# Row scatters tied to TensorE's updates, the expert counts moved by one first product, and a split of the last scaled tile, in a one-core retention + mixture-of-experts kernel

## The chip, the cores and the metric

The kernel runs on one core of a Trainium2 chip. The metric is the device time of one execution in microseconds (us); the lower the better. The engines are TensorE (PE in the profile, its weight loads PEld), VectorE (DVE), ScalarE (ACT), GpSimd (POOL) and SyncE (SP), which here only starts transfers. The kernel's code calls them T, V, A, G and SP.

## The reference, cut to what matters

```python
# q, k, v: [8, 8, 576, 64]
scores = scale * q @ k.transpose(0, 1, 3, 2)
Dmat = where(rel >= 0, gamma[head] ** rel, 0)        # rel = pos_i - pos_j
x = ((scores * Dmat) @ v) -> [4608, 512]             # heads side by side in a row
...
logits = x @ w_gate                                  # 8 experts
e_idx = argmax(logits);  gate_w = softmax(logits)[e_idx]
eom = sigmoid(x @ w_output_gate)
for e in range(8):
    m = e_idx == e
    out[m] = gate_w[m] * eom[m, e] * (relu(x[m] @ w1[e]) @ w2[e])   # F = 1024
```

Every row of x goes through one expert alone, the one with the largest logit.

## The kernel before

The attention works through 36 tiles of 128 rows (NTILE), all heads at once; the loop over g in the manual schedule writes down the order of the instructions of each engine. For tile g TensorE runs: `scores(g + 1)` (32 products of 64x64 on the diagonal block), `by_state(g)` (16 products of the queries with the state that stands for all earlier rows), `outT(g)` (16 products of the masked scores with the values, added to the same PSUM bank `o_ps`), `update(g)` (16 products that add the tile to the state), for about half the tiles `k_rows(g + 1)` (4 transposes), and `xnat(g - 1)` (8 products that turn the tile's result to rows of x and its logits). One tile in nine is without by_state (it begins a sequence), one without update (it ends one).

Beside it VectorE masks the scores (`S_sb`, L384), scales the result (`xT`, L427), does the gate (`gate1a` to `gate4`, for groups of GT = 4 tiles) and part of the split of the weights in two fp32r halves (L153). ScalarE copies the state (`stT`, L402), the keys and the rows of x (`xgrp`, L546) out of PSUM. GpSimd has two things to do in a tile: `prep(g + 1)` (the values scaled by the decay, `vp`, L360), and one indirect DMA of 128 finished rows of x from `xgrp` to their expert's place in `xs` in device memory (`scatter_x`, L200). The scatters of a group stand in the list `todo`; `scatters(n, pause)` takes the next n off it and puts a memset of a 1x1 tile `gap` (L588) ahead of each. That memset is there to wait for GpSimd's own earlier work. Since GpSimd takes its instructions in order, a scatter starts when prep ahead of it is done and its rows are there.

After the tiles come the experts, 8 of them, in two parts of slots each. `mm1(e, part, fb)` makes one block of 128 hidden units: `mm1_products` is 12 products (4 blocks of the inner size, three products of the fp32r halves each) into `h_ps` (L268), `hidden` is relu on ScalarE (L275) and the low half on VectorE (L276). `mm2(e, t)` makes 128 rows of y in `y_ps` by 24 products of 512 columns (L289), ScalarE scales them by the gate (L294) and GpSimd scatters them to the output (L295). Around the end of the attention the counts of rows per expert are made: VectorE finishes `cum` (L518), one small product sums it over partitions (`c_ps`, L734, tile t_ps), and from the copy `cnt` (L735) VectorE works out which slots of `xs` stay empty; GpSimd then fills those with zeros, by scatters with the tile `fill` (L743 and L200).

`pe[0]` is a variable that holds one TensorE instruction; some loads wait for it (`read(paced=...)`). Before, only mm1 and mm2 set it.

## Time and profile before

| what | value |
|---|---|
| median of 3 runs | 603.05 us (602.06 to 604.78) |
| the profiled execution | 606.21 us |
| its span in the trace | 604.40 us |
| TensorE busy | 593.0 us of the span (98%) |
| granted TensorE clock, mean | 0.997 |
| attention | about 0 to 159 us |
| first expert's first blocks, gate of the last group, counts | 159 to 175 us |
| experts | to 597 us |
| last rows scaled and scattered | 597.4 to 600.9 us |

The profile shows one execution on one core. "Busy" of TensorE is modelled from the starts of the products: a stall inside a run of short products shows less in the busy time than in the time from one group's start to the next group's. In the timeline, a row is a run of like instructions: start, length, engine, line, operation, what is written and read, shapes, how many, and in brackets the idle time of that engine before it with what ended it ("issue" where the profile shows no cause).

### The profile page before, as it was taken

The page shows a single profiled execution, that of the slowest core. Times are in us where ns is not written, and L with a number is a line of the kernel's source. Part 1 is how long each engine was busy: PE and PEld are TensorE (multiplying, and loading weights), DVE is VectorE, ACT ScalarE, POOL GpSimd, SP SyncE. Part 2 cuts the span into 40 slices and gives each one's busy share as a digit, 9 for nine tenths or more (in the row PEclk, how much of TensorE's full clock was granted, in tenths as well). Part 3 has the DMA queues.
Part 4 walks back from the last instruction along what each step waited for, and adds up shares of the span by engine and source line. Part 5 has one row for each costly group of instructions (what it writes and reads, how often), then busy time and mean ns, then how long its engine had stood idle before and what let it go on. Part 6 is the DMA issues. An engine that isn't in the chain of part 4 may idle for free. (4 is left out here: it accounts for less than half of the span.)

```text
span 604.4 us, 14010 instructions
## 1 busy us (share of the span) xinstructions
PE 593.0 (98%) x5692; PEld 530.2 (88%) x5692; DVE 330.5 (55%) x731; ACT 226.0 (37%) x502; POOL 189.1 (31%) x235
## 2 busy tenths in 40 slices
PE   8999999999999999999999999999999999999995
PEld 6888888888988999889979987997899799889974
DVE  3588788889650765625543563445265435626410
ACT  4534333234422544325332533443354234325110
POOL 2255454575565624116014301601340110110011
PEclk9999999999999999999999999999999999999998
DMA  8888889887226576435243634434362435221011
GB/s 315 303 307 297 318 300 329 301 278 237 91 106 190 169 207 178 145 102 158 94 133 117 175 109 145 120 122 140 98 192 88 134 96 146 94 84 52 1 39 41
DMA packets 54429, 98.97 MB, mean 164 GB/s; under 512 B 14903, under 2 KB 33336, under 8 KB 54364
## 3 DMA queue, kind: packets, MB, share of 16 engines
q1 hardware_dynamic: 44492, 75.42, 39.2%
q0 software_dynamic: 9440, 21.60, 9.7%
q8 instruction: 45, 0.74, 0.5%
q10 hardware_dynamic: 432, 1.05, 0.4%
q14 instruction: 20, 0.16, 0.1%
HBM read 76.45 MB, written 31.18 MB: 178 GB/s over the span
## 5 line engine op out<-in xcount | busy, mean ns | idle before, releaser
L268 PE MATMUL h_ps<-xh,w1h 128*128 128x360 f32 (+1 forms) x512 | 155.3, 303 | 0.0
L268 PE MATMUL h_ps<-xh,w1l 128*128 128x360 f32 (+1 forms) x512 | 155.0, 303 | 0.0
L268 PE MATMUL h_ps<-xl,w1h 128*128 128x360 f32 (+1 forms) x512 | 154.9, 303 | 0.0
L295 POOL DMA_INDIRECT out_dram<-y,idx x40 | 39.7, 993 | 314.1 <-ACT y L294 268.9
L276 DVE SCALAR_TENSOR_TENSOR hl<-h_ps,hh 128x360 fp32r<-128x360 f32 (+1 forms) x128 | 61.2, 478 | 127.9 <-ACT hh L275 112.5
L289 PE MATMUL y_ps<-w2h,hh 128*128 128x512 f32 (+1 forms) x320 | 124.9, 390 | 0.0
L289 PE MATMUL y_ps<-w2l,hh 128*128 128x512 f32 (+1 forms) x320 | 124.9, 390 | 0.0
L289 PE MATMUL y_ps<-w2h,hl 128*128 128x512 f32 (+1 forms) x320 | 124.6, 389 | 0.0
L275 ACT ACTIVATE hh<-h_ps 128x360 fp32r<-128x360 f32 (+1 forms) x128 | 54.7, 428 | 118.5 <-PE h_ps L268 113.1
L268 PEld LDWEIGHTS h_ps<-xl,w1h 128*128 128x128 f32 x512 | 96.3, 188 | 0.3
L268 PEld LDWEIGHTS h_ps<-xh,w1h 128*128 128x128 f32 x512 | 96.0, 188 | 0.3
L268 PEld LDWEIGHTS h_ps<-xh,w1l 128*128 128x128 f32 x512 | 96.0, 188 | 0.0
L294 ACT ACTIVATE y<-y_ps,idx 128x512 f32<-128x512 f32 (+1 forms) x40 | 27.5, 688 | 138.5 <-issue 90.1
L289 PEld LDWEIGHTS y_ps<-w2h,hl 128*128 128x128 f32 (+1 forms) x320 | 58.8, 184 | 14.1
L289 PEld LDWEIGHTS y_ps<-w2h,hh 128*128 128x128 f32 (+1 forms) x320 | 58.8, 184 | 13.8
L153 DVE TENSOR_TENSOR w1l<-st,w1h 128x512 fp32r<-128x512 f32 x64 | 44.5, 732 | 48.0 <-ACT w1h L148 44.2
L289 PEld LDWEIGHTS y_ps<-w2l,hh 128*128 128x128 f32 (+1 forms) x320 | 58.7, 184 | 13.6
L360 POOL TENSOR_TENSOR vp<-pk,con_sb 128x512 f32<-128x512 f32 x36 | 38.7, 1075 | 56.7 <-PE st_ps L400 35.1
L200 POOL DMA_INDIRECT xs<-zx,fill x42 | 45.9, 1094 | 7.1 <-issue 6.6
L200 POOL DMA_INDIRECT xs<-xgrp,sli x36 | 38.0, 1055 | 29.6 <-issue 10.5
L384 DVE TENSOR_TENSOR S_sb<-sc,con_sb 128x512 f32<-128x512 f32 x64 | 41.1, 683 | 9.5 <-PE sc L373 8.3
L153 DVE TENSOR_TENSOR w2l<-st,w2h 128x512 fp32r<-128x512 f32 x64 | 43.7, 721 | 2.3
(130 smaller groups left out, 683.7 us busy)
## 6 DMA issues: line engine op xcount, KB each, us to landing
st<-in_w_dram SPq DMA_DIRECT2D x64, 512.0 KB
pk<-in_pack_dram SPq DMA_DIRECT2D x32, 768.0 KB
x_q<-xs SPq DMA_DIRECT2D x140, 64.0 KB
kn<-in_krow_dram SPq DMA_DIRECT2D x13, 256.0 KB
pk<-in_pack_dram SPq DMA_DIRECT2D x4, 256.0 KB
pk<-in_pack_dram SPq DMA_DIRECT2D x2, 512.0 KB
x_g<-xs SPq DMA_DIRECT2D x4, 256.0 KB
xs<-zx,fill POOLq DMA_INDIRECT x42
```

Of the source, the lines that this page charges most:

```text
L153: V.tensor_tensor(out=lo[:, k], in0=st[:, k], in1=hi[:, k].bitcast(F32), op=ALU.subtract)
L200: i = G.indirect_dma_start(out=xs, out_offset=bass.IndirectOffsetOnAxis(ap=at, axis=0), in_=x, in_offset=None, **({} if bound is None else ...
L268: i = T.matmul(ps, lhsT=a[:, k, :], rhs=b[:, k, 0:n], start=(j == 0), stop=(j == 3 * KB - 1))
L275: A.activation(out=hh, in_=ps, func=AF.Relu)
L276: V.scalar_tensor_tensor(out=hl, in0=ps, scalar=0.0, in1=hh.bitcast(F32), op0=ALU.max, op1=ALU.subtract)
L289: i = T.matmul(ps, lhsT=a[:, n], rhs=b, start=(j == 0), stop=(j == 3 * FB - 1))
L294: A.activation(out=y, in_=ps, func=AF.Copy, scale=idx.bitcast(F32)[0:m, e, t, 1:2])
L295: G.indirect_dma_start(out=out, out_offset=bass.IndirectOffsetOnAxis(ap=idx[0:m, e, t, 0:1], axis=0), in_=y, in_offset=None, bounds_check= ...
L360: G.tensor_tensor(out=vs[g], in0=pk[g][:, 2].rearrange("p (h d) -> p h d", h=H), in1=gk_sb[:, g % CPB].broadcast_to([P, H, D]), op=ALU.mult)
L384: V.tensor_tensor(out=v(S_sb[:, r].rearrange("p a i -> p (a i)")), in0=v(sc[:, r]), in1=cmat_sb[:, 0:2].rearrange("p c a i -> p a (c i)"). ...
```

## The change

Three edits.

First, update, by_state and outT set `pe[0]` to their last product. `scatters` takes that instruction as a third argument and makes the memset ahead of each scatter wait for it. In the loop a tile's scatter is issued after update(g), no longer ahead of by_state(g); for four tiles (g 27 to 30), which have two scatters, one is issued after by_state(g) and waits for that, the other after update(g). (In a tile without update the last product is outT's.)

Second, the first products of block fb = 5 of expert 0 are issued ahead of the counts' product, and the loop over fb that follows starts at 6.

Third, the last tile of the last expert is scaled in two halves of 256 columns, by ScalarE and VectorE.

```diff
@@ -291,7 +291,11 @@
                     pe[0] = i.ins
                 j += 1
         y = pools["y"].tile([P, DM], F32, name="y")[0:m]
-        A.activation(out=y, in_=ps, func=AF.Copy, scale=idx.bitcast(F32)[0:m, e, t, 1:2])
+        n = DM // 2 if (e, t) == (E - 1, CT - 1) else DM
+        w = idx.bitcast(F32)[0:m, e, t, 1:2]
+        A.activation(out=y[:, 0:n], in_=ps[:, 0:n], func=AF.Copy, scale=w)
+        if n < DM:
+            V.tensor_scalar(out=y[:, n:], in0=ps[:, n:], scalar1=w, scalar2=None, op0=ALU.mult)
         G.indirect_dma_start(out=out, out_offset=bass.IndirectOffsetOnAxis(ap=idx[0:m, e, t, 0:1], axis=0),
                              in_=y, in_offset=None, bounds_check=NT - 1, oob_is_err=False)
 
@@ -397,8 +401,9 @@
         for p in range(NP):
             for r in range(2):
                 o = P * p + 64 * r
-                T.matmul(st_ps[0][64 * r:64 * r + 64, p, :], lhsT=kn[g][lo:P, o:o + D], rhs=vs[g][lo:P, 2 * p + r, :],
-                         start=(c in (0, 4) and p == 0), stop=True, skip_group_check=True)
+                i = T.matmul(st_ps[0][64 * r:64 * r + 64, p, :], lhsT=kn[g][lo:P, o:o + D], rhs=vs[g][lo:P, 2 * p + r, :],
+                             start=(c in (0, 4) and p == 0), stop=True, skip_group_check=True)
+                pe[0] = i.ins
         A.copy(out=stT[g % 2], in_=st_ps[0])
         stcur[0] = stT[g % 2]
 
@@ -412,8 +417,9 @@
             w = 64 if c == 4 else P
             for p, r in order:
                 s = slice(64 * r, 64 * r + 64)
-                T.matmul(part(p, r)[:, 0:w], lhsT=state[s, p, :], rhs=pk[g][s, 0, P * p:P * p + w],
-                         start=(p < 2), stop=False, skip_group_check=True)
+                i = T.matmul(part(p, r)[:, 0:w], lhsT=state[s, p, :], rhs=pk[g][s, 0, P * p:P * p + w],
+                             start=(p < 2), stop=False, skip_group_check=True)
+                pe[0] = i.ins
 
     def outT(g, S_sb, state):
         o = o_ps
@@ -421,8 +427,9 @@
         part = lambda p, r: o[64 * ((p + r) % 2):64 * ((p + r) % 2) + 64, r, P * (p // 2):P * (p // 2) + P]
 
         for r, p in ((r, p) for r in range(2) for p in range(NP)):
-            T.matmul(part(p, r), lhsT=vs[g][:, 2 * p + r, :], rhs=S_sb[:, r, p, :],
-                     start=(state is None and p < 2), stop=True, skip_group_check=True)
+            i = T.matmul(part(p, r), lhsT=vs[g][:, 2 * p + r, :], rhs=S_sb[:, r, p, :],
+                         start=(state is None and p < 2), stop=True, skip_group_check=True)
+            pe[0] = i.ins
         x = wk.tile([P, NP, P], F32, name="xT")
         V.tensor_tensor(out=x.rearrange("p (r s) i -> p r s i", r=2),
                         in0=o[:, :, 0:2 * P].rearrange("p r (s i) -> p r s i", s=2),
@@ -582,10 +589,12 @@
 
     pools["x_ps"] = k_bank
 
-    def scatters(n, pause):
+    def scatters(n, pause, at=None):
         for f in todo[0:n]:
 
-            G.memset(pause, 0.0)
+            i = G.memset(pause, 0.0)
+            if at is not None:
+                tc.add_manual_dep(i.ins, at.name, SYNC, reason="not before TensorE is at this point")
             f()
         del todo[0:n]
 
@@ -614,15 +623,17 @@
             else:
                 pools["x_ps"] = k_bank
                 transp(0, 2)
-            if g < NTILE - 1:
-
-                scatters(2 if GT * SNAP + 6 < g < GT * SNAP + 11 else 1, gap)
             if prev is not None:
                 by_state(g, prev)
+            if GT * SNAP + 6 < g < GT * SNAP + 11:
+                scatters(1, gap, pe[0])
             weights(g)
             if g > 0:
                 outT(g, S_sb, prev)
             update(g)
+
+            if g < NTILE - 1:
+                scatters(1, gap, pe[0])
             if "pend" in gt and g % GT == 2:
 
                 gate2(ps_s.tile([P, NP, P], F32, name="k_ps").rearrange("p a i -> p (a i)"))
@@ -730,8 +741,10 @@
     hidden(*block)
     weights(NTILE)
     weights_lo(NTILE)
+    block = mm1_products(0, 0, 5)
     c_ps = ps_t.tile([P, 512], F32, name="t_ps")[:, 0:E]
     T.matmul(c_ps, lhsT=cbf_sb[:, 1, :], rhs=cum, start=True, stop=True)
+    hidden(*block)
     V.tensor_copy(cnt[:, :, 0], c_ps)
     V.tensor_tensor(out=cnt[:, 0], in0=cnt[:, 0], in1=bump, op=ALU.add)
     fills = fill(0, E, cnt, lim, CT)
@@ -750,7 +763,7 @@
     w = [start_w(1, 1, fp) for fp in range(2)]
     fill_slots(1)
     fill_slots(0)
-    for fb in range(5, FB):
+    for fb in range(6, FB):
         mm1(0, 0, fb)
     load_idx(1, 0)
     load_idx(1, 1)
```

How it moves instructions is shown at three places. GpSimd in the middle of the attention, with the semaphores that each instruction waits for (vp is prep's output, gap the 1x1 tile, xs the rows in device memory); before:

```order
L360 TENSOR_TENSOR vp<-pk,con_sb 128x512 [waits DMAHW0_49,PE_49]
L588 MEMSET gap 1x1 [waits Pool_49]
L200 DMA xs<-xgrp_91,sli 36864x528 [waits DMASW6_49,Activation_49]
L360 TENSOR_TENSOR vp<-pk,con_sb 128x512 [waits DMAHW1_49,PE_49]
L588 MEMSET gap 1x1 [waits Pool_49]
L200 DMA xs<-xgrp_91,sli 36864x528 [waits DMASW7_49,Activation_49]
```

and after:

```order
L364 TENSOR_TENSOR vp<-pk,con_sb 128x512 [waits DMAHW0_49]
L595 MEMSET gap 1x1 [waits PE_49,Pool_49]
L200 DMA xs<-xgrp_91,sli 36864x528 [waits DMASW6_49,Activation_49]
L364 TENSOR_TENSOR vp<-pk,con_sb 128x512 [waits DMAHW1_49]
L595 MEMSET gap 1x1 [waits PE_49,Pool_49]
L200 DMA xs<-xgrp_91,sli 36864x528 [waits DMASW7_49,Activation_49]
```

The rows and their order stay; the wait for TensorE (PE_49) moves from prep to the memset ahead of the scatter, which now stands behind TensorE's update.

TensorE around the counts (t_ps from cum is the counts' product; h_ps_3186 before and h_ps_3125 after are block 5 of expert 0); before:

```order
L268 MATMUL h_ps_3186<-xl0_2779,w1h2_1013 128x360
L268 MATMUL h_ps_3186<-xh0_2778,w1l2_1014 128x360
L268 MATMUL h_ps_3186<-xh0_2778,w1h2_1013 128x360
L268 MATMUL h_ps_3186<-xl0_2779,w1h2_1013 128x360
L734 LDWEIGHTS cbf_sb_82
L734 MATMUL t_ps_3123<-cum_92,cbf_sb_82 128x8
L268 MATMUL h_ps_3186<-xh0_2778,w1l2_1014 128x360
L268 MATMUL h_ps_3203<-xh0_2778,w1h3_1329 128x360
```

and after:

```order
L268 MATMUL h_ps_3125<-xl0_2779,w1h2_1011 128x360
L268 MATMUL h_ps_3125<-xh0_2778,w1l2_1012 128x360
L268 MATMUL h_ps_3125<-xh0_2778,w1h2_1011 128x360
L268 MATMUL h_ps_3125<-xl0_2779,w1h2_1011 128x360
L268 MATMUL h_ps_3125<-xh0_2778,w1l2_1012 128x360
L746 LDWEIGHTS cbf_sb_82
L746 MATMUL t_ps_3138<-cum_92,cbf_sb_82 128x8
L268 MATMUL h_ps_3203<-xh0_2778,w1h3_1327 128x360
```

In the compiled program 11 of the 12 products of block 5 stood ahead of the counts' product already; now all 12 do, so it moves back by one product.

VectorE at the same place (hl_3054 is the low half of block 4, hl_3185 and hl_3124 that of block 5); before:

```order
L518 TENSOR_TENSOR cum<-cum,ohs 128x8
L276 SCALAR_TENSOR_TENSOR hl_3054<-h_ps,hh_3053 128x360
L153 TENSOR_TENSOR w2l_2821<-st,w2h_2820 128x512 x2
L735 COPY cnt<-t_ps 128x8
L276 SCALAR_TENSOR_TENSOR hl_3185<-h_ps,hh_3184 128x360
L736 TENSOR_TENSOR cnt<-cnt,bump 128x1
L213 TENSOR_TENSOR fl<-cnt,csm_sb 128x40
```

and after:

```order
L525 TENSOR_TENSOR cum<-cum,ohs 128x8
L276 SCALAR_TENSOR_TENSOR hl_3054<-h_ps,hh_3053 128x360
L153 TENSOR_TENSOR w2l_2819<-st,w2h_2818 128x512 x2
L276 SCALAR_TENSOR_TENSOR hl_3124<-h_ps,hh_3123 128x360
L748 COPY cnt<-t_ps 128x8
L749 TENSOR_TENSOR cnt<-cnt,bump 128x1
L213 TENSOR_TENSOR fl<-cnt,csm_sb 128x40
```

The copy of the counts out of PSUM (L735, then L748) stands behind the low half of block 5 instead of ahead of it.

At the end of the program ScalarE's last scaling becomes 128x256 instead of 128x512, and VectorE gets one instruction more, of 128x256 (L298).

## Rows read from the trace of the kernel before

**Rows 1.** The page, part 1: busy time of the engines, share of the span, count of instructions.

```profile
PE 593.0 (98%) x5692; PEld 530.2 (88%) x5692; DVE 330.5 (55%) x731; ACT 226.0 (37%) x502; POOL 189.1 (31%) x235
```

**Rows 2.** TensorE's waits by line: idle in total, times, longest.

```profile
PE o_ps L415 <- issue: 1.2, 5, 0.4
```

**Rows 3.** Timeline of all engines, a tile early in the attention, ahead of the first scatter (L373 scores, L415 by_state, L424 outT, L400 update, L402 copy of the state, L437 first step of the gate).

```profile
27.72 0.90 PE L373 MATMUL sc<-pk 64*64 64x128 f32 x32
...
28.44 0.62 PE L415 MATMUL o_ps<-pk,stT 64*64 64x128 f32 x16
28.44 0.19 DVE L437 TENSOR_REDUCE mx<-lg 128x4 f32<-128x32 f32 x1
...
28.99 1.09 PE L424 MATMUL o_ps<-S_sb,vp 128*64 128x128 f32 x16
29.91 0.64 PE L400 MATMUL st_ps<-vp,kn 128*64 128x64 f32 x16
...
30.65 0.37 ACT L402 COPY stT<-st_ps 128x256 f32<-128x256 f32 x1 [2.45 <-PE st_ps L400]
```

**Rows 4.** Timeline of TensorE and GpSimd in a later tile with a scatter (L200).

```profile
77.88 0.90 PE L373 MATMUL sc<-pk 64*64 64x128 f32 x32
...
78.09 1.24 POOL L200 DMA_INDIRECT xs<-xgrp,sli  x1 [0.16 <-ACT xgrp L546]
...
78.60 0.62 PE L415 MATMUL o_ps<-pk,stT 64*64 64x128 f32 x13
...
79.40 0.45 PE L415 MATMUL o_ps<-pk,stT 64*64 64x128 f32 x3 [0.18 <-issue]
...
79.78 0.33 PE L424 MATMUL o_ps<-S_sb,vp 128*64 128x128 f32 x2
```

**Rows 5.** Timeline, the first of nine tiles of that shape.

```profile
47.33 1.01 POOL L200 DMA_INDIRECT xs<-xgrp,sli  x1 [0.16 <-ACT ex L456]
...
48.21 0.92 PE L415 MATMUL o_ps<-pk,stT 64*64 64x128 f32 x16
```

**Rows 6.** Timeline, the last of the nine.

```profile
146.49 1.24 POOL L200 DMA_INDIRECT xs<-xgrp,sli  x1 [0.15 <-ACT kn L356]
...
147.38 0.93 PE L415 MATMUL o_ps<-pk,stT 64*64 64x128 f32 x16
```

**Rows 7.** Timeline of two tiles in which a scatter ran at another place (L360 prep; TensorE is in xnat at 141.25 to 142.33).

```profile
141.17 1.01 POOL L200 DMA_INDIRECT xs<-xgrp,sli  x1 [3.33 <-issue]
...
142.20 1.05 POOL L360 TENSOR_TENSOR vp<-pk,con_sb 128x512 f32<-128x512 f32 x1
142.33 0.90 PE L373 MATMUL sc<-pk 64*64 64x128 f32 x32
...
143.05 0.62 PE L415 MATMUL o_ps<-pk,stT 64*64 64x128 f32 x16
143.19 0.09 POOL L588 MEMSET gap<- 1x1 f32 x1
143.45 1.25 POOL L200 DMA_INDIRECT xs<-xgrp,sli  x1 [0.18 <-issue]
143.60 1.09 PE L424 MATMUL o_ps<-S_sb,vp 128*64 128x128 f32 x16
```

**Rows 8.** Timeline, update, xnat and the next scores of a tile without k_rows, with a scatter beside them (xnat runs between the two PE rows).

```profile
38.27 0.63 PE L400 MATMUL st_ps<-vp,kn 128*64 128x64 f32 x16
38.72 1.15 POOL L200 DMA_INDIRECT xs<-xgrp,sli  x1 [2.63 <-PE o_ps L424]
...
40.01 0.90 PE L373 MATMUL sc<-pk 64*64 64x128 f32 x32
```

**Rows 9.** Timeline of a tile with two scatters.

```profile
122.75 1.01 POOL L200 DMA_INDIRECT xs<-xgrp,sli  x1 [2.34 <-ACT w2h L148]
...
124.06 0.96 POOL L200 DMA_INDIRECT xs<-xgrp,sli  x1 [0.21 <-issue]
...
124.47 0.89 PE L373 MATMUL sc<-pk 64*64 64x128 f32 x26
...
125.58 0.38 PE L373 MATMUL sc<-pk 64*64 64x128 f32 x6 [0.22 <-issue]
```

**Rows 10.** Timeline at the counts (L518 the last sum over a group, L734 the counts' product).

```profile
172.29 0.33 PE L268 MATMUL h_ps<-xh,w1h 128*128 128x360 f32 x1
...
172.45 0.33 PE L268 MATMUL h_ps<-xl,w1h 128*128 128x360 f32 x1
...
173.09 0.17 DVE L518 TENSOR_TENSOR cum<-cum,ohs 128x8 bf16<-128x8 bf16 x1
...
173.31 0.18 PE L734 MATMUL t_ps<-cum,cbf_sb 128*128 128x8 bf16 x1 [0.53 <-DVE cum L518]
```

**Rows 11.** Timeline, the table of empty slots on VectorE and the first scatter that reads it on GpSimd.

```profile
177.19 0.20 DVE L224 TENSOR_TENSOR fill<-fl,csm_sb 128x40 int32<-128x40 f32 x1
...
179.24 1.00 POOL L200 DMA_INDIRECT xs<-zx,fill  x1 [0.30 <-DVE hl L276]
```

**Rows 12.** Timeline, the end of the program.

```profile
597.41 0.69 ACT L294 ACTIVATE y<-y_ps,idx 128x512 f32<-128x512 f32 x1 [4.75 <-PEq L813]
598.37 0.98 POOL L295 DMA_INDIRECT out_dram<-y,idx  x1 [4.44 <-ACTq L813]
```

**Rows 13.** The group of instructions of this shape: count, busy time, mean ns of one, idle before.

```profile
L276 DVE SCALAR_TENSOR_TENSOR hl<-h_ps,hh 128x256 fp32r<-128x256 f32 x64 | 27.1, 424 | 51.8 <-ACT hh L275 38.5 <-issue 13.3
```

## The prediction

> **What bounds the kernel now.** I read the busy times first: TensorE is busy for 593.0 of 604.4 us [rows 1], so only what delays TensorE itself can move the end, apart from the few us after its last product. Then TensorE's waits: they name by_state (L415) with 1.2 us of idle time in five places and "issue" as the cause, that is, no cause [rows 2]. That figure is too small, because the ends of products are modelled. So I went to the timeline and measured from the start of one group to the start of the next. In an undisturbed tile scores take 28.44 − 27.72 = 0.72 us and by_state 28.99 − 28.44 = 0.55 us [rows 3]. In the tile at 77.88 scores are as long, but by_state takes 79.78 − 78.60 = 1.18 us: 13 products run, the other three only from 79.40 on [rows 4]. On GpSimd a row scatter started at 78.09 and lasted 1.24 us, to 79.33; TensorE goes on 0.07 us after its end. Nine tiles have this shape, the first at 48.21 [rows 5] and the last at 147.38 [rows 6]; in each a scatter overlaps scores and ends after by_state has begun. The excess over the usual length goes from 0.28 to 0.76 us, and the nine together lose 4.26 us.
>
> A scatter elsewhere costs nothing. The one at 141.17 lies beside xnat, the one at 143.45 begins in the middle of by_state and covers outT, and scores (0.72), by_state (0.55) are as in the quiet tile [rows 7]. The difference that the rows show is a count. From the scatter's start to its end, 22 products of scores and 13 of by_state started at 78.09, then TensorE stood; at 146.49 it was some 40 before it stood. Scores issue one product in 0.0225 us, by_state one in 0.034, outT one in 0.057, xnat one in 0.15 at most, so only a scatter over scores and by_state meets so many. No scatter in the trace saw more than 41 products start, and a single scatter with fewer than 34 stalled none.
>
> **Part 1, the held scatters.** The row order on GpSimd stays; only the point at which the scatter may start moves. What others see as the end of update is the copy of the state: it starts 30.65 − 29.91 = 0.74 us after update's first product [rows 3]. Call that U. The memset starts there and the scatter 143.45 − 143.19 = 0.26 us later [rows 7], and it lasts 1.01 to 1.25 us [rows 5, 7], so it runs from U + 0.26 to U + 1.27, at worst U + 1.51. With k_rows the next scores start about 1.4 us after U: the scatter is over, or nearly. Without k_rows (some 12 of the tiles with a scatter) they start 40.01 − 38.27 − 0.74 = 1.0 us after U [rows 8]. There the scatter covers the last five products of xnat and 12 to 23 of scores, 17 to 28 in all, and ends ahead of by_state, which begins at U + 1.72. That is below the least count of 34 at which a tile stalled. I take 0.05 us for each of the 12, since such a tile is not in the trace (from below none, from above 0.30, the price of the mildest stalls [rows 6]): +0.6, between 0 and +3.6. The removed stalls give −4.26.
>
> The four tiles with two scatters lose too. At 122.75 and 124.06 two run with a gap of 0.3 us, scores stop after 26 products and go on at 125.58, about 0.5 us late [rows 9]; a second place like it lies in the next tile. Together that is about 1.1 us. After the change the first of a pair covers outT and update, the second starts some 0.3 us behind it, and xnat is done as it ends in tiles with k_rows; in the two without, scores may stall by 0 to 0.5 us. I take half: 0.5 us lost instead of 1.1, so −0.6, between 0 and −1.1.
>
> What is queued behind the new wait is prep(g + 2) on GpSimd. Prep used to start as soon as update freed its tile; now it starts behind the scatter, at about U + 1.3, and takes 1.05 us [rows 7], so it ends at U + 2.4. It is needed by the outT after the next, about one and a half tiles after U, that is some 6 us: 3.6 us of cover, so nothing. If that cover were gone, each late us would be a us of TensorE in up to 30 tiles. The loads of keys and packs on SyncE wait for none of this. A scatter later by 1 to 3 us has until the row buffer is rewritten, about three tiles later; nothing there is near.
>
> **Part 2, the counts.** TensorE issues a product every 0.16 us here (172.29, 172.45), and then stands 0.53 us, until the last sum over the group is there (173.09 + 0.17) [rows 10]. The compiled order puts one more product ahead, not a block, so 0.17 of the 0.53 us is filled: −0.17, between 0 and −0.2; 0.36 us of the wait stays. The copy of the counts goes behind one more low half on VectorE, 0.5 us. Its reader, the first scatter of zeros, starts at 179.24, 1.85 us after the table it needs (177.19 + 0.20) [rows 11], since the row scatters ahead of it hold GpSimd; that covers the 0.5 us. Without that cover the zeros would be later, not TensorE.
>
> **Part 3, the last tile.** ScalarE takes 0.69 us at 597.41 and the scatter starts 0.27 us after it ends [rows 12]. A half of 256 columns on VectorE, also reading PSUM, took 0.424 us [rows 13]; ScalarE's half is no longer. So the scatter can start 0.27 us earlier, at best 0.3, at worst at no gain if the second wait costs as much: −0.27, between 0 and −0.3.
>
> **Sum.** −4.26 + 0.6 − 0.6 − 0.17 − 0.27 = −4.7 us. After the counts the view of TensorE's waits names no line more, so what is won before shifts the end by as much. The profiled execution of 606.21 would become 601.5; against the median of 603.05 it gives 598.3 us.
>
> **Rivals.** (a) The hold gains nothing, because by_state's stall is not the scatter's doing. In the stalled tiles VectorE begins a group's gate at that point, as at 28.44 (L437), and the excess could come from there. Then parts 2 and 3 alone are left: 603.05 − 0.44 = 602.6. Against it: the tile of [rows 3] has the same gate rows, no scatter and the usual 0.55 us; and in [rows 4] TensorE resumes at the scatter's end. A rule of the Trainium skill (SBUF — State Buffer, section "SBUF: two separate sides") speaks for this rival: of the engines' ports only the pair that VectorE shares with GpSimd is contended, and TensorE never waits on anyone. By that a scatter could not hold TensorE and the time would be this rival's; rows 4 to 6 do not agree with it, if port conflicts are what is meant.
>
> (b) Slower. A scatter stalls whatever short products run beside it, and fixing it to update moves all 30 to a place where it always meets some. By the median stall of 0.5 us that is 30 × 0.5 = 15, less 4.3 and 0.4: +10.3, 613.4 us. It decides from (4.26 + 0.44) / 30 = 0.16 us a scatter. Against it: the scatters beside xnat and beside update in [rows 7, 8] and seven more like them left tiles of the usual length.
>
> (c) The 12 tiles without k_rows pay the upper price: +3.6 instead of +0.6, the sum is −1.7 and the time 601.3. For it speaks only that no tile shows just this overlap; against it the count above.
>
> **How the numbers follow.** Forecast 598.3 with chance 0.63 (its own range, from the bounds of the terms with the spread of the runs, 596 to 600.2); (a) 0.20; (c) 0.10; (b) 0.07. The range reaches from 596.0 over (c) and (a) to 602.7; (b) and the ends of the forecast are left out, about 0.15. A measurement of this kernel can tell about 0.5%, 3.0 us, from no change. Faster by more than that (under 600.0) is nearly all of the forecast and a little of (c): 0.64; within it 0.29; slower 0.07.
>
> **What would show it right or wrong.** In the profile after, the scatters begin about 0.26 us after the memset, which begins with the copy of the state; by_state takes 0.55 us in the tiles that now take 0.83 to 1.3; TensorE's wait at the counts shrinks from 0.53 to some 0.36 us; the last row scatter starts some 0.7 us after ScalarE begins its last scaling, instead of 0.96. If scores or xnat are longer by what by_state lost, (b) or (c) holds; if by_state is still long with no scatter beside it, (a). The forecast fails if prep comes late, which outT would show with a wait for vp, or if VectorE becomes what TensorE waits for in the attention.

## The result, and the profile after

The changed kernel is **slower**, by about 1%: 608.99 us median (607.50 to 609.87) against 602.86 us (600.91 to 604.78) for the kernel before on the same chip, a ratio of 1.0097 with a 95% interval of 1.0074 to 1.0119. Forecast was 598.3 us. The time lies outside the range and on the side to which I gave 0.07.

The two profiled executions differ by less: 608.19 against 606.21 us, because the one of before lies 3.35 us above its median and the one of after 0.80 us below. So ratios are taken from the timed runs, and places from the traces. The 1.98 us between the traces lie in three places. The first expert's first product starts at 160.97 instead of 159.51 us (+1.46), the stretch from the last products of the group's gate to the second layer takes 7.11 instead of 6.89 us (+0.22), and from the last product to the last scatter it is 1.74 instead of 1.44 us (+0.30). By the starts of TensorE's groups the +1.46 us is a sum of large terms: by_state takes 4.3 us less and scores 0.5 less, update 2.5 more, xnat 2.5, the gate's products 1.1 and the transposes ahead of the experts 0.3. So in this trace the forecast saving at by_state came, and more than that was lost behind it. For part 1 the trace of the experiment that has it alone (below) shows more: there the first product starts at 163.40, 3.89 us late.

Busy times of after, part 1 of the page, answering to [rows 1]: TensorE has lost 2.6 us of busy time in a longer span, and VectorE has gained 9.2 us (from 330.5) with one instruction more.

```profile
PE 590.4 (97%) x5692; PEld 528.8 (87%) x5692; DVE 339.7 (56%) x732; ACT 226.8 (37%) x502; POOL 187.8 (31%) x235
```

TensorE's waits by line (total us, times, longest), answering to [rows 2]. The five places of by_state with no named cause are gone. In their place stand waits on VectorE: for the mask of the scores, which frees their bank (S_sb, L388), for the copy of the gate's logits (L558) and for the low half of x (L251). With the two short ones it is 5.7 us; before it was 0.2.

```profile
PE sc L377 <- DVE S_sb L388: 2.4, 9, 0.7
PE xa L549 <- DVE lg L558: 1.7, 2, 1.2
...
PE k_ps L471 <- DVE xl L251: 1.1, 1, 1.1
PE t_ps L746 <- DVE cum L525: 0.7, 1, 0.7
...
PE o_ps L430 <- DVE S_sb L388: 0.3, 1, 0.3
PE sc L377 <- DVE S_sb L385: 0.2, 1, 0.2
```

Busy time by engine from 25 to 150 us (TensorE, weight loads, VectorE, ScalarE, GpSimd), first of before, then of after: TensorE loses 2.7 us, VectorE gains 6.65 with three instructions fewer. Its operations have become longer.

```profile
25.00:150.00 125.00, 123.03 (x2581) 108.86 (x2582) 106.76 (x309) 45.26 (x126) 65.06 (x90) 1.00 0.86 301
```

```profile
25.00:150.00 125.00, 120.33 (x2582) 107.50 (x2583) 113.41 (x306) 46.24 (x126) 62.95 (x88) 1.00 0.85 300
```

The timeline of after at six places (start, length, engine, line, operation):

```profile
54.97 0.09 POOL L595 MEMSET gap<- 1x1 f32 x1 [1.84 <-PE st_ps L404]
...
55.73 1.01 POOL L200 DMA_INDIRECT xs<-xgrp,sli  x1 [0.66 <-ACT stT L407]
...
77.67 1.01 POOL L200 DMA_INDIRECT xs<-xgrp,sli  x1 [0.68 <-ACT stT L407]
77.87 0.90 PE L377 MATMUL sc<-pk 64*64 64x128 f32 x32
78.07 2.24 DVE L153 TENSOR_TENSOR w1l<-st,w1h 128x512 fp32r<-128x512 f32 x1
78.59 0.62 PE L420 MATMUL o_ps<-pk,stT 64*64 64x128 f32 x16
78.70 1.05 POOL L364 TENSOR_TENSOR vp<-pk,con_sb 128x512 f32<-128x512 f32 x1
79.14 1.10 PE L430 MATMUL o_ps<-S_sb,vp 128*64 128x128 f32 x16
...
146.76 2.22 DVE L153 TENSOR_TENSOR w2l<-st,w2h 128x512 fp32r<-128x512 f32 x1
...
151.60 1.19 DVE L453 TENSOR_TENSOR fst<-fst,csm_sb 128x32 f32<-128x32 f32 x1
151.69 1.05 POOL L364 TENSOR_TENSOR vp<-pk,con_sb 128x512 f32<-128x512 f32 x1
...
154.98 0.69 DVE L251 TENSOR_TENSOR xl<-k_ps,xh 128x512 fp32r<-128x512 f32 x1 [0.31 <-ACT xh L247]
...
155.73 0.18 PE L471 MATMUL k_ps<-oh,cbf_sb 128*128 128x32 bf16 x1 [1.14 <-DVE xl L251]
...
160.97 0.42 PE L268 MATMUL h_ps<-xh,w1h 128*128 128x360 f32 x1
...
173.93 0.17 DVE L497 CAST sli<-slf 128x4 int32<-128x4 f32 x1 [0.95 <-DMA xs<-zx,fill]
...
175.15 0.18 PE L746 MATMUL t_ps<-cum,cbf_sb 128*128 128x8 bf16 x1 [0.74 <-DVE cum L525]
...
598.61 0.39 PE L289 MATMUL y_ps<-w2h,hl 128*128 128x512 f32 x1
599.08 0.47 ACT L296 ACTIVATE y<-y_ps,idx 128x256 f32<-128x256 f32 x1 [4.75 <-PEq L826]
599.59 0.48 DVE L298 TENSOR_SCALAR y<-y_ps,idx 128x256 f32<-128x256 f32 x1 [21.67 <-ACT y L296]
600.35 0.98 POOL L299 DMA_INDIRECT out_dram<-y,idx  x1 [4.74 <-DVE y L298]
```

What to see. The tile at 77.87 answers to [rows 4]: by_state takes 0.55 us again (78.59 to 79.14). At 54.97 the scatter starts 0.76 us after its memset, where [rows 7] have 0.26 us; the median over the held scatters is 0.75 us. Prep now starts 0.02 us behind the scatter's end (78.70), inside scores and by_state. In that time VectorE's low half of the expert's weights (L153), 0.68 us when nothing lies beside it, takes 2.24. At 146.76 the low half takes 2.22 us (0.95 in before) and puts VectorE behind. So at 151.60 it comes late to a step of the gate, 0.18 us when alone, which takes 1.19 and ends with prep. In before this step takes 0.99 us, but is done 0.8 us ahead of the next scores. What follows from it (gate, copies of the rows, high and low half of x) comes late, and TensorE stands 1.14 us at 155.73. The rows at 173.93 and 175.15 answer to [rows 10], the last three to [rows 12].

### The profile page after: what moved, and what is told of

Same layout as the page of the kernel before. It is cut to its first block, busy times and chain, and to the rows that moved or that the text cites. A ratio compares the mean times of both kernels' runs of the same rounds, so it can differ in the third digit from the quotient of the medians.

```text
span 606.3 us, 14019 instructions
## 1 busy us (share of the span) xinstructions
PE 590.4 (97%) x5692; PEld 528.8 (87%) x5692; DVE 339.7 (56%) x732; ACT 226.8 (37%) x502; POOL 187.8 (31%) x235
## 3 DMA queue, kind: packets, MB, share of 16 engines
q10 hardware_dynamic: 432, 1.05, 0.4%
## 5 line engine op out<-in xcount | busy, mean ns | idle before, releaser
L296 ACT ACTIVATE y<-y_ps,idx 128x512 f32<-128x512 f32 (+2 forms) x40 | 27.3, 683 | 138.5 <-issue 90.1
L153 DVE TENSOR_TENSOR w1l<-st,w1h 128x512 fp32r<-128x512 f32 x64 | 47.4, 777 | 48.0 <-ACT w1h L148 46.6
L200 POOL DMA_INDIRECT xs<-zx,fill x42 | 45.0, 1071 | 8.2 <-issue 7.1
L153 DVE TENSOR_TENSOR w2l<-st,w2h 128x512 fp32r<-128x512 f32 x64 | 45.2, 744 | 2.3
L200 POOL DMA_INDIRECT xs<-xgrp,sli x36 | 37.3, 1036 | 27.2 <-ACT stT L407 13.3
L388 DVE TENSOR_TENSOR S_sb<-sc,con_sb 128x512 f32<-128x512 f32 x64 | 41.0, 681 | 7.4 <-PE sc L377 7.4
```

The lines of the kernel that those rows point to most:

```text
L153: V.tensor_tensor(out=lo[:, k], in0=st[:, k], in1=hi[:, k].bitcast(F32), op=ALU.subtract)
L200: i = G.indirect_dma_start(out=xs, out_offset=bass.IndirectOffsetOnAxis(ap=at, axis=0), in_=x, in_offset=None, **({} if bound is None else ...
L296: A.activation(out=y[:, 0:n], in_=ps[:, 0:n], func=AF.Copy, scale=w)
L388: V.tensor_tensor(out=v(S_sb[:, r].rearrange("p a i -> p (a i)")), in0=v(sc[:, r]), in1=cmat_sb[:, 0:2].rearrange("p c a i -> p a (c i)"). ...
```

## The experiments

Each ratio is to the kernel before on the same chip, with its 95% interval; for e1 to e15 that kernel's median there was 605.8 to 607.3 us. "Stretch" is worked out from the trace: over all VectorE rows that start between 25 and 150 us, length less the shortest row of the same line. "Held" counts the VectorE rows of that window that start ahead of a prep, last into it and are lengthened by over 0.2 us. "VectorE" is the busy time in that window.

| run | what | ratio | stretch, us | held | VectorE, us |
|---|---|---|---|---|---|
| before | | 1 | 12.7 | 2 | 106.8 |
| after | | 1.0097 [1.0074, 1.0119] | 22.4 | 13 | 113.4 |
| e1 | part 1 alone | 1.0071 [1.0045, 1.0097] | 24.5 | 15 | 113.3 |
| e2 | parts 2 and 3 alone | 1.0012 [0.9998, 1.0026] | 12.7 | 2 | |
| e3 | before, prep later | 0.9985 [0.9968, 1.0001] | 8.7 | 1 | 103.8 |
| e4 | before, scatter after scores | 0.9956 [0.9936, 0.9976] | 14.0 | 3 | |
| e5 | after, prep on ScalarE | 0.9954 [0.9933, 0.9974] | 1.3 | 0 | 98.2 |
| e6 | after, scatter itself waits | 1.0051 [1.0032, 1.0069] | 21.0 | 11 | |
| e7 | e4, scatter itself waits | 0.9937 [0.9915, 0.9959] | 14.7 | 2 | 109.2 |
| e8 | before, prep on ScalarE | 1.0409 [1.0337, 1.0480] | 0.8 | 0 | |
| e9 | prep after scores, then scatter | 0.9971 [0.9956, 0.9987] | 11.6 | 0 | |
| e10 | e7, prep on ScalarE | 0.9929 [0.9902, 0.9956] | 1.0 | 0 | 97.8 |
| e11 | e7 with parts 2 and 3 | 0.9951 [0.9934, 0.9968] | 12.5 | 2 | |
| e12 | e7 with part 2 | 0.9956 [0.9939, 0.9972] | 13.0 | 2 | |
| e13 | part 1, prep moved away | 0.9969 [0.9957, 0.9981] | 8.1 | 0 | 102.7 |
| e14 | scatter after scores, then prep | 0.9971 [0.9957, 0.9986] | 14.0 | 3 | 109.8 |
| e15 | e14, prep after outT | 0.9963 [0.9944, 0.9981] | 14.3 | 3 | 110.7 |

Three theories are put to the test. Theory P: prep's new place lets it shut VectorE's operations out, and TensorE waits for VectorE. Theory S: the scatters at their new place hold TensorE up. Theory R: parts 2 and 3 cost.

**Which part: e1 and e2.** e1 is the change without its first and last two pieces, e2 is those alone. The core of e1, and of e2:

```
-            if g < NTILE - 1:
-
-                scatters(2 if GT * SNAP + 6 < g < GT * SNAP + 11 else 1, gap)
...
             update(g)
+
+            if g < NTILE - 1:
+                scatters(1, gap, pe[0])
```

```
+    block = mm1_products(0, 0, 5)
...
+    hidden(*block)
```

> Part 1 of the change alone. Theory P (the held scatter pushes prep behind it, to where VectorE works on two SBUF inputs; the two exclude each other and VectorE becomes the bound): all of the loss and a little more, about 609.3 us, ratio 1.010 to 1.012. Theory S (the scatter at its new place, beside update and xnat, makes TensorE's ends visible late and delays VectorE and ScalarE; prep plays no part): the same 609.3. Theory R (the loss comes from parts 2 and 3): 598 to 603 us.

> Parts 2 and 3 alone. Theories P and S: 602.4 us (0.17 us at the counts and 0.27 us at the end, not to be told from no change). Theory R: 606 us or more.

Part 1 carries most of the loss: 1.0071 alone. Parts 2 and 3 together cost about 0.7 us at an interval that reaches zero; theory R is at most a small share. In e1's trace, unlike after's, by_state still stalls as well: between 40 and 150 us it loses 3.7 us, against 4.6 in before and 0.2 in after, though the scatters are held to the same point. The timeline of e1 at 81.7 us shows the chain of one loss from end to end:

```profile
81.73 1.01 POOL L200 DMA_INDIRECT xs<-xgrp,sli  x1 [0.66 <-issue]
...
82.34 1.54 DVE L449 TENSOR_TENSOR fst<-fst,csm_sb 128x32 f32<-128x32 f32 x1
82.77 1.05 POOL L360 TENSOR_TENSOR vp<-pk,con_sb 128x512 f32<-128x512 f32 x1
...
83.91 0.19 DVE L451 TENSOR_REDUCE m<-fst 128x4 f32<-128x32 f32 x1
...
84.59 0.18 DVE L457 TENSOR_REDUCE zs<-zo 128x4 f32<-128x32 f32 x1
...
84.81 0.20 ACT L460 ACTIVATE zs<-zs 128x4 f32<-128x4 f32 x1 [2.63 <-DVE zs L457]
...
85.31 0.17 DVE L554 COPY lg<-xa 128x16 f32<-128x16 f32 x1 [0.53 <-ACT xgrp L549]
85.54 0.64 PE L545 MATMUL xa<-iw,xT 128*128 128x144 f32 x3 [0.60 <-DVE lg L554]
```

A step of 0.18 us starts in the middle of a scatter and 0.43 us ahead of prep, and is done when prep is done, 1.36 us later than alone. The gate's steps stand behind it. ScalarE waits for their sum (L460) before it copies the rows of x, VectorE's copy of the logits (L554) follows on that, and TensorE waits 0.60 us for this copy. (The last row shows three of the four products of its group.)

**Is prep merely late? e3.** Before, with prep held to the last product of xnat of the tile ahead:

```
-        G.tensor_tensor(out=vs[g], in0=pk[g][:, 2].rearrange("p (h d) -> p h d", h=H),
+        i = G.tensor_tensor(out=vs[g], in0=pk[g][:, 2].rearrange("p (h d) -> p h d", h=H),
...
+        if xn[0] is not None and 8 < g < NTILE:
+            tc.add_manual_dep(i.ins, xn[0].name, SYNC, reason="not before TensorE is at this point")
```

> The kernel before with prep alone held, until xnat of the tile before is issued (from tile 9 on); scatters follow prep as before, so that they fall beside outT and update and the by_state stalls should go too. Theory P: as slow as the changed kernel, 606 to 610 us, with VectorE's split of the weights at 1.3 us or more a piece instead of 1.04. Theory S: faster, about 599 us, since no scatter stands beside xnat and the 4.3 us of stalls are gone.

The ratio, 0.9985, is no change. Prep starts 0.16 us after scores' start here, where in after it is 0.47 us (medians), so even its place within the tile is nearly that of after. TensorE waits nowhere for vp or for VectorE between 25 and 160 us, so that being late costs nothing there, as the prediction said, and P in its simple form falls. What e3 lacks is a scatter directly ahead of prep; the stretch is smaller, 8.7 us. The ratio is not the price of prep's place alone, though: the scatters follow prep, by_state loses 1.2 instead of 4.6 us, and TensorE stands 2.6 us with no named cause in scores, by_state and update instead.

**Does prep matter at all? e5 and e8.** Prep as a copy on ScalarE, in after (e5) and in before (e8). The copy leaves out the decay factor, so these kernels do less than the reference asks; they serve to see what prep's place on GpSimd costs.

```
-        G.tensor_tensor(out=vs[g], in0=pk[g][:, 2].rearrange("p (h d) -> p h d", h=H),
-                        in1=gk_sb[:, g % CPB].broadcast_to([P, H, D]), op=ALU.mult)
+        A.copy(out=vs[g], in_=pk[g][:, 2].rearrange("p (h d) -> p h d", h=H))
```

> The changed kernel with prep taken off GpSimd: ScalarE copies the values instead (the decay factor is left out, so that the output differs from the reference). The held scatters stay as in the changed kernel. Theory P (VectorE's operations with two SBUF inputs and GpSimd's prep exclude each other, and the hold moves prep onto them): VectorE's split of the weights back to 0.69 us a piece from 1.35, its busy time of 25 to 150 us about 113 us on the scale on which the changed kernel has 127, and the kernel faster than before by 4 to 5 us (ratio 0.992). Theory S (the scatter at its new place is what costs): no better than the changed kernel, ratio 1.007 to 1.010.

> The kernel before with prep on ScalarE as in e5 (decay factor left out), scatters not held. Control for e5: VectorE free of collisions, but scatters as they come. Theory P with the stalls as read from the trace of before: between no change and 3 us faster, worse than e5 by what the scatters over scores still cost. If the hold were worth nothing and only the collisions counted: as fast as e5.

e5 takes away the whole loss and 0.46% more: held scatters without prep on GpSimd are faster than before. e8 goes the other way, 4.1% slower, for a reason of its own. With prep gone nothing spaces the scatters, and they come one behind another. Timeline of e8:

```profile
59.80 1.47 POOL L200 DMA_INDIRECT xs<-xgrp,sli  x1 [0.22 <-issue]
...
60.69 1.10 PE L372 MATMUL sc<-pk 64*64 64x64 f32 x31
...
61.58 0.96 POOL L200 DMA_INDIRECT xs<-xgrp,sli  x1 [0.23 <-issue]
62.17 0.21 PE L372 MATMUL sc<-pk 64*64 64x64 f32 x1 [0.38 <-issue]
62.20 0.43 PE L414 MATMUL o_ps<-pk,stT 64*64 64x128 f32 x3
...
62.85 0.96 POOL L200 DMA_INDIRECT xs<-xgrp,sli  x1 [0.22 <-ACT xgrp L545]
62.93 0.46 PE L414 MATMUL o_ps<-pk,stT 64*64 64x128 f32 x3 [0.30 <-issue]
63.69 0.44 PE L414 MATMUL o_ps<-pk,stT 64*64 64x128 f32 x5 [0.31 <-issue]
```

By_state goes on three to five products at a time, and stands while scatters run. So prep between the scatters also did a service in the kernel before, and it is confirmed that a scatter can hold TensorE; the count of products that pass is no fixed one.

**Is it the place of the scatter? e4, e6, e7.** e4 is before with its scatters, where they stand in the code, held to the last product of the scores beside them; e7 puts the wait on the scatter instead of the memset; e6 does that in after, at update.

```
+        sp[0] = i.ins
...
-                scatters(2 if GT * SNAP + 6 < g < GT * SNAP + 11 else 1, gap)
+                scatters(2 if GT * SNAP + 6 < g < GT * SNAP + 11 else 1, gap, sp[0])
```

The wait on the scatter itself, in e6 and e7:

```
+            if at is not None:
+                tc.add_manual_dep(scat[-1], at.name, SYNC, reason="not before TensorE is at this point")
```

> The kernel before with each scatter held to the last product of the next scores, prep left where it was (right behind update). Theory P: by_state at 0.55 us in every tile, VectorE's busy time as before, 598 to 599 us (4.3 us of stalls gone). Theory S: 602 us or more, because the scatter beside outT makes its end visible late to VectorE, which needs it for xT. If the stalls in the trace of before were worth nothing: 602.9.

> The changed kernel with the wait for TensorE on the scatter itself instead of the memset ahead of it, so that GpSimd has the scatter ready when TensorE is done. In the changed kernel the scatter began 0.66 us after its memset. If that gap is the price of waking up after a wait, scatter and prep now start some 0.4 us earlier; by theory P prep then hits fewer of VectorE's operations: ratio 1.000 to 1.005. By theory S, or if the gap stays: 1.007 to 1.010.

> The kernel with scatters held to the next scores (e4), the wait on the scatter itself instead of the memset. By theory P the scatter ends about 0.4 us earlier, prep starts right at the end of update beside VectorE's work on PSUM, and the rest of the gain comes: ratio 0.990 to 0.994 (e4 had 0.9956). If the start of the scatter does not move: 0.9956 again.

Held to scores the scatters gain, 0.44 and 0.63%, and by_state's loss between 40 and 150 us falls from 4.6 us to 0.4 and 0.6; held to update they lose, with the wait in either form. In e6 the scatter starts only 0.1 us sooner (median, from update's start): the late start is not the memset's doing. e4 and e7 can't be told apart by their intervals.

**How much is prep worth once the scatters stand well? e9 and e10.** e9 is before with prep(g + 1) behind the scores and held to their last product, the scatter behind it; e10 is e7 with e5's copy. The core of e9:

```
-                prep(g + 1)
                 S_next = scores(g + 1)
+                prep(g + 1, sp[0] if g >= 8 else None)
```

> The kernel before with prep held to the last product of the next scores, about 0.9 us later than in e3; the scatter follows it and falls beside outT and update, not held itself. VectorE then masks the scores out of PSUM, which takes no second SBUF input. Theory P in its sharper form (what counts is which of VectorE's operations lie beside prep, not that prep is late): VectorE's stretch below 9 us (12.7 in before, 22.5 in the changed kernel, 8.7 in e3), by_state at 0.55, ratio 0.990 to 0.995. If lateness of prep itself costs (outT waits for vp): 1.005 or more, with waits of outT for vp in the trace.

> Prep on ScalarE as in e5 (decay factor left out) and the scatters held to the next scores as in e7: neither collisions nor scatters over scores. By theory P with both effects added, the sum of what is to be had in this stage: ratio 0.987 to 0.991. If e5 was limited by something else than scatters over scores (e5 still has by_state at 0.6 to 1.0 in a dozen tiles): 0.9954 as e5.

e9 gained 0.3%, less than expected, with prep lengthening the gate's small steps there (six of one line took 0.65 us more each). e10 beats e7 by less than either interval. In after, taking prep off GpSimd is worth 1.4% (e5), in e7 0.1%, and e10's hoped-for sum of both effects (0.987 to 0.991) did not come: the cost is not prep's and not the scatter's alone, but of the two together at that place.

**Parts 2 and 3 on the better kernel: e11, e12.** e7 with both (e11) and with part 2 (e12).

> e7 with parts 2 and 3 of the change: the hold at another point, the rest as changed. e7 had 0.9937; parts 2 and 3 alone 1.0012 with an interval that holds 0. Expected 0.992 to 0.995.

> e7 (scatters held to the next scores, wait on the scatter) with part 2 but without part 3, since the traces so far show part 3 as a loss of 0.3 us at the end (VectorE's half begins when ScalarE's is done) and part 2 as a gain of about 0.16 us between the gate's last products and the second layer. Expected 0.992 to 0.995, the last scatter 1.44 us after TensorE's last product again instead of 1.74, and 6.7 us instead of 6.9 from the last first-layer block of the gate to the first second-layer product, if the zero fill lands as early as it does in e11.

Neither is faster than e7. In both traces the stretch from the gate's last products to the second layer is 6.73 to 6.74 us instead of 6.89, so part 2 gives its 0.15 us in traces where VectorE doesn't wait for the zeros to land; with the whole tile scaled by ScalarE (e12), last product to scatter is 1.43 us as before.

**Queueing behind the scatter, or the place? e13, e14, e15.** e13 is e1 with prep(g + 1) put behind the next scores and held to their end, so that it no longer stands directly behind a running scatter. e14 is before with the scatter held to scores and prep directly behind it; e15 the same with prep held to outT's last product.

The core of e13 is e9's two lines in e1. The core of e14, and the line that e15 has in place of its last:

```
-                prep(g + 1)
                 S_next = scores(g + 1)
+                if g < NTILE - 1:
+                    scatters(2 if GT * SNAP + 6 < g < GT * SNAP + 11 else 1, gap, sp[0])
+                prep(g + 1)
```

```
+            if 8 <= g < NTILE - 1:
+                prep(g + 1, sp[1])
```

> Part 1 alone (each scatter held to the last product of update, as in e1), with prep(g+1) put behind the next scores in GpSimd's order and held to the last product of those scores, so that prep no longer stands directly behind a running scatter. Queueing (Q: what costs is that a VectorE operation that comes while prep waits behind a running scatter is shut out from then until prep's end): no operation of 0.16 to 0.19 us is held from before prep starts, VectorE's stretch between 25 and 150 us falls from e1's 24.5 to 9 to 13 us, and the ratio to the kernel before is 0.993 to 1.000, where e1 had 1.007. If what costs is the place of the scatter, or prep being late: 1.005 or more, as e1.

> The kernel before, with each scatter held to the last product of the scores that stand beside it and prep directly behind the scatter in GpSimd's order. Queueing (Q): operations of 0.16 to 0.19 us are held from before prep starts until its end, the stretch is over 16 us, and the kernel is slower than e9, which has the same two in the other order (0.997): ratio 1.000 to 1.008. If the order of the two on GpSimd does not matter: about e9's 0.997 or lower, and a stretch near e9's 11.6 us.

> As e14, but prep(g+1) is put behind outT of the same tile and held to the last product of outT, so that it starts 0.3 us or more after the scatter has ended. Queueing (Q): no operation is held from before prep starts, the stretch is below 13 us and the ratio 0.992 to 0.998, lower than e14's. If the distance between the two does not matter: the same as e14 within 0.2%.

e13 keeps the scatters where e1 has them and turns 1.0071 into 0.9969: the loss of part 1 is prep's place behind them, whole. No VectorE step is held from ahead of prep there (15 in e1). Prep is later than in e1 too, some 1.2 instead of 0.5 us after scores' start, so e13 by itself does not part the queueing from the place. Its low halves all take 0.67 to 0.71 us. Timeline of e13, the tile that answers to the one at 77.87 above:

```profile
76.37 0.09 POOL L596 MEMSET gap<- 1x1 f32 x1 [0.89 <-PE st_ps L405]
76.43 0.68 DVE L153 TENSOR_TENSOR w1l<-st,w1h 128x512 fp32r<-128x512 f32 x1
...
77.12 1.01 POOL L200 DMA_INDIRECT xs<-xgrp,sli  x1 [0.66 <-ACT stT L408]
77.34 0.90 PE L377 MATMUL sc<-pk 64*64 64x128 f32 x32
...
78.06 0.83 PE L421 MATMUL o_ps<-pk,stT 64*64 64x128 f32 x16
...
78.68 1.03 POOL L360 TENSOR_TENSOR vp<-pk,con_sb 128x512 f32<-128x512 f32 x1 [0.55 <-PE sc L377]
```

By_state takes 0.21 us too long here (0.83 in the row, 0.62 in a quiet tile), since the scatter, which starts 0.75 us after its memset, reaches into it.

e14 missed. It has prep 0.03 us behind the scatter and the same ratio as e9, 0.9971, where I expected 1.000 or more. Timeline of e14:

```profile
91.51 1.01 POOL L200 DMA_INDIRECT xs<-xgrp,sli  x1 [0.66 <-issue]
...
92.55 1.05 POOL L360 TENSOR_TENSOR vp<-pk,con_sb 128x512 f32<-128x512 f32 x1
92.83 1.33 DVE L153 TENSOR_TENSOR w1l<-st,w1h 128x512 fp32r<-128x512 f32 x1
```

Here too the low half is lengthened, in 12 of 14 cases, to 1.17 to 1.71 us. But ten of the twelve begin 0.16 to 0.44 us after prep, so that prep simply came first, and nearly all lie at the tile's end, 3 us and more after scores' start, where nothing that TensorE waits for stands close behind: TensorE's waits on VectorE in the attention are 0.5 us. The holding from ahead of prep, which the expectation rested on, occurs three times in e14: beside the scatters VectorE mostly reads PSUM at that place (S_sb, xT), and those rows take 0.68 us as ever. So e14 hardly tried the queueing, rather than showing it to be harmless. Over all runs the count goes with the loss: after, e1 and e6 have 11 to 15 such steps and lie above 1.005, no other run has more than three, and of those only e8 lies clearly above 1. That is an agreement over 17 traces; the sizes of the three losses don't follow the count. e15 says nothing on the distance: since the scatter starts 0.75 us late, outT's end came before the scatter's, and prep started 0.03 us behind it as in e14.

## Why the prediction was wrong, step by step

- **The stall of by_state is the scatter's doing: right.** With the scatters held to scores (e4, e7) it is all but gone, in after too, and in e8 scatters hold TensorE everywhere. Rival (a) is out. (Against the quiet time of each form of by_state, 0.55 us and 0.34 with 64 columns, the nine stalls add up to 4.5 us rather than 4.26.) The same rows go against the Trainium skill (SBUF — State Buffer, section "SBUF: two separate sides") where it says that TensorE never waits on anyone, if port conflicts are what is meant.
- **"3.6 us of cover, so nothing" for prep: the step that failed.** That prep is late for outT costs nothing: in e3 and e13 TensorE never waits for vp. But I asked only who waits for prep, not what it does to others while it runs. Its new place is inside the next scores, directly behind a running scatter. Steps of VectorE with two operands in SBUF (L153 and the gate's) that begin shortly ahead of it end with prep or 0.56 us after it, at 1.2 to 2.2 us instead of 0.16 to 0.68. Behind them stand the mask of the scores and the gate's chain, and TensorE waits 5.7 us on VectorE, more than the 4.3 us that by_state gives back. e5 and e13 each undo the cause and the loss goes with it. The sentence that names VectorE among the ways to fail was right, and no term stood for it. The same section of the Trainium skill says that VectorE and GpSimd share a port pair with an exclusive lock, which goes to whichever starts first; I drew on its other half. The traces agree in that L153 is never longer than 0.75 us where prep is not on GpSimd (e5, e8, e10). On who goes first they don't agree with it: the 13 steps held in after began ahead of prep. The price could be read before the change, beside the two scatters of [rows 9], where prep follows a scatter directly. A VectorE step of 0.16 us took 1.75 there and ended with prep:

```profile
124.37 1.75 DVE L223 TENSOR_TENSOR fl<-fl,fo 128x3 f32<-128x3 f32 x1
...
125.05 1.05 POOL L360 TENSOR_TENSOR vp<-pk,con_sb 128x512 f32<-128x512 f32 x1
```

- **"The scatter starts 0.26 us after the memset": mis-sized.** It is 0.75 us (median of the held scatters), where it now comes after a wait. By U + 0.26 (U is the start of the copy of the state) the scatter was to be over before by_state; by U + 0.75 it isn't. What that costs differs from trace to trace. Between 40 and 150 us by_state loses 0.2 us in after, against 4.6 in before, but 3.7 and 2.8 in e1 and e6, which hold the scatters at the same point, and 3.8 and 2.7 in e5 and e13, where VectorE is free. So in these four the −4.26 shrinks to 0.8 to 1.9 us. Why after's trace is spared stays open: TensorE comes late to by_state there, held up by VectorE, but in e1 and e6 VectorE holds it up as well, for 3.6 and 3.0 us.
- **The 12 tiles without k_rows, 0.05 us each:** no stall of scores there, as said. Rival (c) is out.
- **Two-scatter tiles, −0.6:** not gained; about 1.6 us are lost instead of 1.2, in the waits behind update and xnat.
- **Part 2, −0.17:** the product that is put ahead gives 0.15 to 0.16 us (e5, e11, e12). In after and e2 it is lost again, +0.22 and +0.57, because a small cast of VectorE in front of the last sum waits for the landing of the zero rows (173.93), a wait that I had covered by the engine's time alone. That wait is not part 2's doing: e1, e13 and e15, which are without part 2, have it too (7.55, 7.63 and 7.22 us for the stretch of 6.89). What brings it on stays open.
- **Part 3, −0.27:** wrong, +0.30. VectorE's half starts 0.04 us after ScalarE's ends, not beside it. Both read y_ps, one bank. The Trainium skill (PSUM — Partial Sum Buffer, section "PSUM bank collisions raise a hardware error") states that two engines may not be at one bank and quadrant at once, reads included; the row agrees that they were ordered. Both also write one tile y, and no run tells which of the two ordered them. Two halves of 0.47 and 0.48 us one after the other are longer than the whole at 0.69.
- **Rival (b)** had the sign and not the mechanism: in after scatters hardly stall what they lie beside, VectorE holds TensorE up. In e1 and e6 they do stall by_state, but no more than in before.

## What to carry to other kernels

When an instruction is held, follow what is queued behind it to its new place and ask what it does there to the engines that share a port with it, not only who waits for it. A chain that has room on its own engine (VectorE at 85% in this stretch) can still set TensorE's pace if two or three of its steps grow to twice their length or more just ahead of what TensorE needs. Here the hold is right at another point: after the scores, with prep left at the tile's end, it gives 0.9937 (e7), against 1.0097 at update.

## What the runs showed of the hardware that was not expected

- A VectorE step with two operands in SBUF that starts in the last 0.7 us of a scatter on GpSimd, with prep queued directly behind the scatter, stands still until prep's end: steps of 0.19 us took 1.48 us at 99.06 and 1.67 us at 115.98 in after, one of 0.18 took 1.54 at 82.34 in e1. Over the 17 traces 59 such steps, begun 0.06 to 0.73 us ahead of prep, were all held, and seven begun 0.75 to 1.0 us ahead of it were not (98.63 and 115.54 in after, 0.17 and 0.19 us). Steps that read PSUM (S_sb, xT) were not lengthened. A scatter alone does not do this (in e13 ten low halves of L153 beside scatters take 0.67 to 0.71 us), and in e13 no step is held from before prep's start. That prep takes the port when it is queued rather than when it starts is my reading of it, argued and not shown.
- Where VectorE starts first and no scatter lies directly ahead, it is prep that waits: in before L153 takes 0.68 us with prep beginning 0.2 us into it, and that prep 1.36 instead of 1.05 us (106.97 and 107.19).
- A scatter that follows a wait of GpSimd's starts about 0.75 us after its memset, one that follows work 0.25 us (medians of after and before). The cause stays open; a wait on the scatter itself does not remove it (e6).
- TensorE issues some 34 to 41 short products from a scatter's start before it stands, in before; in e13 42 to 44, in after 45 in one scatter (94.66) without standing; in e8, with scatters one behind another, three to five. So the count that the prediction drew on is no limit by itself.
- In e7, e10 and e14 TensorE loses 0.3 to 1.2 us at each of two places, about 56 and 74 us, with no scatter beside it, in e10 and e14 some 0.5 more at 140 us. The cause stays open; no run tests it.
